# Attention and a gated feed-forward layer on one core: a sixth block of P per pair transposed by DMA, and the order of steps worked out anew

## The chip, the core and the metric

The kernel runs on one core of a Trainium2 chip. The core has a matrix engine (TensorE, PE in the profile; its weight loads are PEld), three elementwise engines (VectorE = DVE, ScalarE = ACT, GpSimd = POOL) and SyncE (SP), which in this kernel issues all DMA transfers. The five run side by side, each through its own instructions in order. The metric is the time of one execution on the device in microseconds (us), less is better.

## The reference

```
q_n, k_n = rmsnorm(q, g_q), rmsnorm(k, g_k)          # over head_dim
scores = (1 / sqrt(64)) * q_n @ k_n^T                # 8 batches x 12 heads, 448 x 448
attn = softmax(scores);  x = attn @ v                # heads joined: 8 x 448 x 768
h = relu(x @ w_in)                                   # 768 -> 1024
c[t] = cw[0]*h[t-1] + cw[1]*h[t] + cw[2]*h[t+1]      # three taps along the sequence
out = (h * sigmoid(c)) @ w_out                       # 1024 -> 768
```

All inputs of the attention are float32; the three weights of the second part arrive as 64-bit floats. The output is float32, 8 x 448 x 768.

## The kernel before

**Tiling.** Two heads make a pair, so there are 48 pairs, six for each batch. The 2 x 448 = 896 query rows of a pair are cut into seven blocks of 128 rows (`SLOTS`, `NS = 7`), numbered `j = 0..6` in the order in which they are worked on. Float32 values on the matrix path are split in two float16 halves, a high and a low one (`hi = cast(x)`, `lo = x - hi`), and a product is three float16 matmuls. Pairs 0 to 9 (`whole(n)`, `PH["nf"] = 10`) use float32 matmuls without the split.

**Steps of a pair.** `load_k`, `load_q`, `v_load` bring the data. `square`, `square_sum`, nine `rsqrt` steps and `apply_rms` (lines 385 to 441) normalise q and k. k, and q of the first ten pairs, are turned on TensorE (`qk_transpose`), evacuated and split; q of pairs from ten on is split first (`q_hi`, `q_lo`) and turned by a DMA transpose (`q_turn`). For each of the seven blocks `scores` does the matmuls, `soft_max` the row maximum on DVE, `soft_exp` the exponential on ACT with the row sum beside it. The result is P, 128 rows x 448 columns in float32, and P has to be turned, since P times V sums over the columns. There are two ways for it:

- on TensorE: `p_transpose` (line 686, four transposes into a PSUM bank), `p_evac` (cast of the bank to the high half, on ACT or DVE), `p_low` (line 702, the low half on DVE);
- by DMA: `p_hi` (cast to the high half in one of four buffers `ph`), `p_lo` (the low half, line 110), `p_turn` (line 678, one DMA transpose of both halves, SBUF to SBUF, issued by SP).

`nd(n)` says how many of the seven blocks go by DMA: none for pairs below `PH["n1"] = 10`, and `PH["nd"] = 5` for the others, since `PH["n2"] = 0`. So before, blocks 0 to 4 of pairs 10 to 47 go by DMA, 38 x 5 = 190 transposes, and blocks 5 and 6 go through TensorE. Both ways write the same tile `PT`, of which there are two; a `p_hi` needs a free one of the four `ph` buffers, that is, the transpose of four turns before has landed. `pv` (line 764) multiplies `PT` by the split V, `x_scale`, `x_hi`, `x_lo` divide by the row sums and split again. The row sums take a way of their own through DRAM (`sum_add` to `sum_load`, lines 709 to 729).

**Steps of a batch.** When the six pairs of a batch are there, `in_part` (line 848) multiplies by w_in, `in_relu`, `in_conv`, `in_tanh`, `in_gate`, `in_hi`, `in_lo` make the gated product, and `out_part` (line 917) multiplies by w_out.

**The order.** No step waits in source order: every step is entered in a plan with a due time (`at(t, fn, ...)`, shifted by `SHIFT`), what it needs (`needs`), and what it costs on each engine that may do it (`options`). Before the program is built, a planner goes through simulated time. For each engine it picks the step with the smallest sum of its earliest start and `beta` times its urgency, and it picks the engine where there is a choice (`on[step]`, with a patience `PH["p_..."]` for the second engine). `PH` holds the limits too: `nbulk`, how many bulk loads may be in flight, `cs`, `ct`, `cm`, how many PSUM banks each use may hold. The result is one fixed order for each engine. The times in `options` enter only this order; on the chip each engine runs its list in order and waits on semaphores.

```
key = t + sw + (BETA if e != "SP" else PH["sp"]) * urgency(step), urgency(step), steps[step][1]
if pick is None or key < pick[0]:
    pick = key, t, step
```

Of the kernel before, what the change touches and what calls it, by code (L numbers as in the profile page):

```python
# [17 lines left out]


PH = dict(  # L20
    sw=0.0, f_pl=0.0, f_ql=1.033, f_lo=0.063, f_rms=0.006, f_sq=0.0, T=17.289, ti=32.944,
    si=4.255, so=8.682, hop=0.426, beta=0.03, wi0=-31.45, wi1=127.539, wo0=29.304, wo1=182.047,
    cw=74.737, p_evac=1.025, p_hi=0.642, p_lo=3.777, p_rms=17.798, p_v=0.759, p_x=3.533,
    p_g=0.165, p_relu=0.299, p_cv=2.053, p_ev=3.086, sp=0.027, nbulk=6, p_rs=0.095, p_sq=3.551,
    p_w=3.55, v0=13.758, nd=5, cs=5, ct=4, cm=9, ne=5, n2=0, n1=10, q1=10, nf=10, pvs=4,
    p_sa=3.242, p_c0=3.399, p_ca=1.542, p_ss=0.242, p_qh=2.3, p_ql=2.401, p_ph=0.99, p_pl=1.378,
)
PACE = [
    17.644, 18.636, 16.286, 18.384, 14.587, 14.007, 12.166, 11.326, 21.435, 16.597, 21.428,
    21.065,  # L30
]
SHIFT = dict(
    prepare=-80.692, load_g=44.746, make_g=210.801, load_cw=-19.035, make_cw=387.553,
    load=41.371, convert=225.692, bound=365.257, bound_max=324.412, bound_turn=42.238,
    bound_row=76.875, bound_spread=4.635, scale=275.319, in_factor=440.833, split=103.321,
    rest=-2.799, out_factor=-0.968, load_k=306.569, load_q=-19.17, square=439.405,
    square_sum=329.986, rsqrt=54.627, apply_rms=238.269, qk_transpose=264.997, qk_hi=82.963,
    v_load=445.045, v_bound=-0.71, scores=57.55, soft_max=-4.441, soft_exp=50.335,
    p_transpose=316.253, p_evac=1.763, sum_add=226.657, sum_step=5.685, sum_transpose=51.88,
    sum_evac=233.745, sum_store=120.158, sum_load=1.259, pv=451.756, x_scale=158.975,  # L40
    x_hi=114.608, x_lo=5.331, v_max=-19.522, v_turn=600.483, v_row=7.16, v_spread=215.011,
    v_scale=11.299, qk_lo=-6.348, q_hi=-9.487, q_lo=109.312, q_turn=418.088, p_hi=567.012,
    p_lo=0.249, p_turn=241.201, p_low=3.084, v_hi=86.801, v_lo=289.452, moe_scales=90.042,
    in_part=33.426, in_relu=242.776, in_conv=118.288, in_tanh=106.186, in_gate=-5.208,
    in_hi=235.807, in_lo=15.201, in_carry=67.828, out_scales=27.298, out_part=423.396,
    out_evac=97.431, out_store=-1.54,
)
SCHED = {}
ON_ACT = ""
# [20 lines left out]
def tile_attention_moe(ctx: ExitStack, tc, q, k, v, g_q, g_k, w_in, conv_w, w_out, out):  # L70
# [15 lines left out]
    T = PH["T"]  # L86
# [79 lines left out]
    cw = cw_in if conv_w.dtype == F32 else const.tile([P, 3, NFC], F32, name="cw")  # L166
# [3 lines left out]
    wo = wo32.bitcast(F16).rearrange("p c (s e) -> p s c e", s=2)  # L170
# [438 lines left out]
    def nd(n):  # L609
        return 0 if n < PH["n1"] else PH["ne"] if n < PH["n2"] else PH["nd"]  # L610
# [663 lines left out]
    def options(name, *a):  # L1274
        n, wo = a[0] if a else None, a and a[0] == "out"
        n0 = a and isinstance(a[0], int) and a[0] < 2
        dma = lambda kind, c, k=1, g="C": ("ACT" if kind in ON_ACT.split() else "SP", c, (g, k))
        dve, act, pool, pe = (lambda c, e=e: (e, c, None) for e in ("DVE", "ACT", "POOL", "PE"))
        return dict(
            load=lambda: [dma("w", 1.5 if wo else 1.95)],  # L1280
            convert=lambda: [dve(0.55 if wo else 0.68)] if a[2] else [dve(0.35 if wo else 0.42)],
            bound=lambda: [act(0.6 if wo else 0.7)],
            bound_max=lambda: [dve(0.1)],
            scale=lambda: [dve(0.6)],
            split=lambda: [act(0.94 if wo else 1.15)],
            rest=lambda: [dve(1.01 if wo else 1.28), pool(3.9 if wo else 4.95)],
            in_factor=lambda: [dve(0.07)],
            out_factor=lambda: [dve(0.07)],
            load_g=lambda: [dma("g", 0.3, 4)],
            make_g=lambda: [dve(0.36)],  # L1290
            prepare=lambda: [dve(0.1)],
            load_cw=lambda: [dma("cw", 0.55)],
            make_cw=lambda: [dve(0.52)],
            load_k=lambda: [dma("lk", 0.82)],
            load_q=lambda: [dma("lq", 0.53, 2) if n % 2 else dma("lq", 1.05)],
            square=lambda: [act(1.06), pool(1.89)] if a[1] == 2 else [act(0.55), pool(1.05)],
            square_sum=lambda: [dve(1.21 if a[1] == 2 else 0.62)],
            rsqrt=lambda: [dve(0.19)] if a[1] == 1 or n0 and not a[2] else [dve(0.19), pool(0.47 if a[1] in (4, 7, 8) else 0.23)],
            apply_rms=lambda: [dve(0.69), pool(1.04)] if n0 else [pool(1.04), dve(0.69)],
            qk_transpose=lambda: [pe(0.42)],  # L1300
            qk_hi=lambda: [act(0.6), dve(0.62)],
            qk_lo=lambda: [dve(0.65)],
            q_hi=lambda: [act(0.62), dve(0.42), pool(0.61)],
            q_lo=lambda: [pool(1.15), dve(0.69)],
            q_turn=lambda: [("SP", 1.25, ("T", 1))],
            v_load=lambda: [dma("lv", 0.78)],
            v_bound=lambda: [dve(0.68)],
            v_max=lambda: [dve(0.3)],
            v_scale=lambda: [dve(0.7)],
            scores=lambda: [pe(0.77 if whole(a[0]) else 0.585)],  # L1310
            soft_max=lambda: [dve(0.62)],
            soft_exp=lambda: [act(0.73)],
            p_transpose=lambda: [pe(0.455)],
            p_low=lambda: [dve(0.63)],
            p_evac=lambda: [act(0.59), dve(0.62)],
            sum_add=lambda: [pool(0.3), dve(0.09)],
            sum_step=lambda: [dve(0.195)],
            sum_store=lambda: [dma("rd", 0.2)],
            sum_load=lambda: [dma("rb", 0.45)],
            pv=lambda: [pe(0.765 if nd(a[0]) else 8 * 0.00086 * S)],  # L1320
            x_scale=lambda: [dve(0.7 if nd(a[0]) else 0.85)],
# [24 lines left out]
            v_lo=lambda: [dve(0.75)],
            p_hi=lambda: [act(0.57), dve(0.39), pool(0.55)],
            p_lo=lambda: [pool(1.03), dve(0.61)],
            p_turn=lambda: [("SP", 1.25, ("T", 1))],
        )[name]()  # L1350

    PATIENCE = dict(
        qk_hi="hi", q_hi="qh", q_lo="ql", apply_rms="rms", x_hi="x", x_lo="lo", in_hi="g", in_lo="g",
        out_evac="ev", sum_add="sa", v_hi="hi", v_lo="lo", p_hi="ph", p_lo="pl", sum_evac="ev", v_bound="v", rest="w", rsqrt="rs", square="sq", convert="c0", in_relu="relu", in_conv="cv", p_evac="evac", in_carry="ca",
# [117 lines left out]
    while len(order) < len(steps):  # L1472
        best, free_banks = None, room()
        for e, ws in waiting.items():
            pick = None
            for step, (t, _, dma) in ws.items():
# [29 lines left out]
        _, c, dma = waiting[e][step]  # L1506
# [82 lines left out]
```

## Time and profile before

| | us |
|---|---|
| median of three runs | 846.53 (845.52 to 847.14) |
| the profiled execution | 847.59 |
| its span, first to last instruction | 845.8 |

The page of the profile gives the busy time of each engine over the span, the span in 40 slices, the DMA queues, the chain of work that ended last and the costliest groups of instructions. A group's line names the source line, engine, operation, written and read tiles, shapes and count; then its busy time and the mean duration of one in ns; then the idle time of the engine before them and who ended it. A table by stages gives, for each stretch of the span, the busy time of the engines, the granted clock of TensorE, and the share of the 16 DMA engines.

In 40 slices, the tenths of busy time of the engines and of the DMA:

```profile
PE   4897999999999999999999999999899999999998
DVE  6998999997999988897699997897899877883430
ACT  4988998898899888898899887898899887883541
POOL 1352665587787865877787864876788775862110
DMA  8954545259987899589986899589987997484001
```

The last three slices or so are the feed-forward part of the last batch alone, on TensorE.

### The profile page before, as it was taken

Reading aid. Unit: us, or ns where it says so; the run is one execution under the profiler, and the core shown is the slowest. Engines: PE = TensorE matmul, PEld = TensorE weight load, DVE = VectorE, ACT = ScalarE, POOL = GpSimd, SP = SyncE. Lnnn points to the kernel's source line nnn. Section 1 sums busy time; section 2 is a strip of 40 time slices with the busy share of each in tenths; the row PEclk is TensorE's granted clock in tenths of the full one; section 3 lists DMA queues with packets and bytes.
Section 4 is the critical chain, followed back from the end, with each engine's and each line's share of the span. In section 5 each row is a group of like instructions: output and inputs, shape, how many; then the busy total and the mean of one; then the engine's idle time right before and its main releaser. Section 6 shows DMA issues by size and latency. Waiting matters only on the chain.

```text
span 845.8 us, 17137 instructions
## 1 busy us (share of the span) xinstructions
PE 807.7 (95%) x5726; PEld 441.5 (52%) x5726; DVE 692.6 (82%) x1303; ACT 693.0 (82%) x1622; POOL 533.5 (63%) x649
## 2 busy tenths in 40 slices
PE   4897999999999999999999999999899999999998
PEld 2443545445555555555555555555555555555554
DVE  6998999997999988897699997897899877883430
ACT  4988998898899888898899887898899887883541
POOL 1352665587787865877787864876788775862110
PEclk9998999999999999999999999999999999999999
DMA  8954545259987899589986899589987997484001
GB/s 205 237 155 119 137 144 156 70 93 188 190 179 137 174 192 203 110 168 170 212 184 139 173 185 189 115 173 179 207 179 151 166 175 149 79 144 116 10 16 60
DMA packets 305576, 127.50 MB, mean 151 GB/s; under 512 B 245248, under 2 KB 301904, under 8 KB 305488
## 3 DMA queue, kind: packets, MB, share of 16 engines
q1 hardware_dynamic: 305488, 126.41, 71.8%
q8 instruction: 45, 0.74, 0.4%
q14 instruction: 43, 0.35, 0.2%
HBM read 56.65 MB, written 11.18 MB: 80 GB/s over the span
## 4 chain that ended last, share of the span: by engine, by line
PE 42%; DVE 22%; DMA 12%; ACT 10%; POOL 6%; issue 4%; SPq 3%; ACTq 0%; POOLq 0%; DVEq 0%
PE bank L848 15%; PE bank L917 13%; PE bank L764 5%; DMA PT<-ph 5%; PE bank L642 5%; PE bank L686 3%; DMA rB<-rd 2%; POOL ph L110 2%; DMA wo<-in_moe_w_in_dram 2%; DMA qkf<-in_q_dram 2%; POOL sq L110 2%; DVE st L396 1%; ACT ph L98 1%; DVE vp L748 1%; DVE PT L702 1%
## 5 line engine op out<-in xcount | busy, mean ns | idle before, releaser
L848 PE MATMUL bank<-x,wi 128*128 128x448 f16 x1152 | 233.4, 353 | 0.0
L917 PE MATMUL bank<-wo,gring 128*128 128x384 f16 (+1 forms) x1056 | 196.5, 327 | 0.0
L848 PEld LDWEIGHTS <-wi 128*128 128x128 f16 x1152 | 110.1, 98 | 101.6 <-issue 10.3
L642 PE MATMUL bank<-kT,qT 64*128 64x448 f16 (+3 forms) x1072 | 132.0, 395 | 4.0 <-ACT qT L98 2.6
L917 PEld LDWEIGHTS <-gring 128*128 128x128 f16 (+1 forms) x1056 | 101.6, 99 | 63.1 <-issue 8.8
L110 POOL TENSOR_TENSOR sq<-qkf,st 112x512 f32<-112x512 f32 x92 | 101.1, 1115 | 6.1 <-DVE st L417 5.0
L764 PE MATMUL bank<-PT,vp 112*64 112x448 f16 x912 | 93.5, 354 | 0.0
L110 POOL TENSOR_TENSOR x<-x,x 128x448 f16<-128x448 f32 x48 | 50.5, 1052 | 54.8 <-ACT x L98 53.9
L764 PEld LDWEIGHTS <-vp 112*64 112x64 f16 x912 | 48.5, 110 | 40.2 <-issue 10.8
L396 DVE TENSOR_REDUCE st<-sq 112x16 f32<-112x1024 f32 (+1 forms) x50 | 58.3, 1167 | 12.3 <-ACT sq L385 12.1
L702 DVE TENSOR_TENSOR PT<-bank,PT 112x512 f16<-112x512 f32 x76 | 51.5, 682 | 11.5 <-ACT PT L98 11.4
L642 PEld LDWEIGHTS <-qT 64*128 64x128 f16 (+1 forms) x912 | 33.3, 97 | 48.7 <-issue 27.3
L385 ACT ACTIVATE sq<-qkf 112x1024 f32<-112x1024 f32 (+1 forms) x47 | 48.2, 1025 | 11.7 <-DMA qkf<-in_q_dram 6.6
L98 ACT CAST PT<-bank 112x512 f16<-112x512 f32 x76 | 44.2, 583 | 3.9 <-PE bank L686 3.8
L917 PE MATMUL bank<-wo,wi 128*128 128x384 f16 (+1 forms) x192 | 46.9, 326 | 0.0
L456 PE MATMUL bank<-ident,sq 112*128 112x112 f32 x232 | 33.8, 270 | 13.6 <-DVE st L425 9.1
L748 DVE SCALAR_TENSOR_TENSOR vp<-v,vsc,vp 112x512 f16<-112x512 f32 x38 | 40.3, 1060 | 5.5 <-ACT vp L102 5.4
L110 POOL TENSOR_TENSOR qkf<-sq,qkf 112x512 f16<-112x512 f32 x35 | 42.3, 1209 | 0.2
L98 ACT COPY PT<-bank 112x512 f32<-112x512 f32 x69 | 39.5, 582 | 2.3 <-PE bank L686 2.1
L709 POOL TENSOR_SCALAR rsum<-rsum 128x7 f32<-128x7 f32 x48 | 14.5, 302 | 42.1 <-ACT e_(0_6_304 L656 10.7
L775 DVE TENSOR_TENSOR x<-bank,rB 128x448 f32<-128x448 f32 x38 | 23.5, 620 | 18.5 <-PE bank L764 11.8
L764 PE MATMUL bank<-PT,v 112*64 112x448 f32 x160 | 33.9, 568 | 3.6 <-ACT PT L98 3.4
(2228 smaller groups left out, 1972.9 us busy)
## 6 DMA issues: line engine op xcount, KB each, us to landing
qkf<-in_k_dram SPq DMA_DIRECT2D x48, 224.0 KB
v<-in_v_dram SPq DMA_DIRECT2D x48, 224.0 KB
rB<-rd SPq DMA_DIRECT2D x96, 112.0 KB
wo<-in_moe_w_in_dram SPq DMA_DIRECT2D x12, 512.0 KB
gring<-in_moe_w_out_dram SPq DMA_DIRECT2D x16, 384.0 KB
qkf<-in_q_dram SPq DMA_DIRECT2D x24, 224.0 KB
qkf<-in_q_dram SPq DMA_DIRECT2D x48, 112.0 KB
PT<-ph SPq DMA_TRANSPOSE x190
```

Source lines behind the costliest of these rows:

```text
L98: (nc.scalar.copy if e == "ACT" else elementwise(e).tensor_copy)(dst, src)
L110: elementwise(e).tensor_tensor(dst, a, b, op=op)
L385: nc.scalar.activation(sq, x, AF.Square)
L396: nc.vector.tensor_reduce(st, sq, axis=AX.X, op=ALU.add)
L456: nc.tensor.transpose(ps[:, t * PB : (t + 1) * PB], x[:, t], ident[:PB, :PB])
L642: nc.tensor.matmul(ps[u][o, :S], lhs, rhs, start=(i == 0), stop=(whole(m) or i == 2),)
L686: nc.tensor.transpose(ps[:PB, kt * P : (kt + 1) * P], e[:, kt * PB : (kt + 1) * PB], ident)
L702: nc.vector.tensor_tensor(turned(n, j, 1), held["t", ("p", n, j)][:PB].rearrange("p (k q) -> p k q", k=NB), turned(n, j, 0), op=ALU.subtract,)
L748: nc.vector.scalar_tensor_tensor(vp[:, 1], old("v", n), old("vsc", n // NP)[:PB, 1:2], vp[:, 0], op0=ALU.mult, op1=ALU.subtract,)
L764: nc.tensor.matmul(ps[HALF[h], :S], lhs, rhs, start=(i == 0 and k == 0), stop=(i == pvs(n)[-1] and k == NB - 1),)
L848: nc.tensor.matmul(ps[:, :S], wi[:, wl, c, fc * P : (fc + 1) * P], old("x", b * NP + c)[:, xl], start=(i == 0), stop=(i == 3 * NP - 1),)
L917: nc.tensor.matmul(ps[p0 : p0 + m, :NO2], g, wo[:, wl, fc, half * NO2 : (half + 1) * NO2], start=(i == 0), stop=(i == 3 * NFC - 1),)
```

## The change

`PH["nd"]` goes from 5 to 6 (and `ne`, which no pair uses while `n2 = 0`): block 5 of pairs 10 to 47 takes `p_hi`, `p_lo`, `p_turn` in place of `p_transpose`, `p_evac`, `p_low`. Block 6 stays on TensorE. Beside it the figures of `options` are set to other durations, and all numbers of `PH`, `PACE` and `SHIFT`, from which the planner makes its order, are new. No function is added, and no computation changes.

```diff
 PH = dict(
-    sw=0.0, f_pl=0.0, f_ql=1.033, f_lo=0.063, f_rms=0.006, f_sq=0.0, T=17.289, ti=32.944,
-    si=4.255, so=8.682, hop=0.426, beta=0.03, wi0=-31.45, wi1=127.539, wo0=29.304, wo1=182.047,
+    sw=0.0, f_pl=0.0, f_ql=0.616, f_lo=0.065, f_rms=0.079, f_sq=0.356, T=17.368, ti=37.602,
+    si=4.258, so=8.922, hop=0.87, beta=0.015, wi0=-40.604, wi1=121.264, wo0=30.91, wo1=183.564,
...
-    p_g=0.165, p_relu=0.299, p_cv=2.053, p_ev=3.086, sp=0.027, nbulk=6, p_rs=0.095, p_sq=3.551,
-    p_w=3.55, v0=13.758, nd=5, cs=5, ct=4, cm=9, ne=5, n2=0, n1=10, q1=10, nf=10, pvs=4,
+    p_g=6.911, p_relu=3.009, p_cv=2.979, p_ev=1.037, sp=0.047, nbulk=3, p_rs=0.08, p_sq=9.733,
+    p_w=34.001, v0=27.558, nd=6, cs=5, ct=4, cm=8, ne=6, n2=0, n1=10, q1=10, nf=10, pvs=4,
...
-            load=lambda: [dma("w", 1.5 if wo else 1.95)],
-            convert=lambda: [dve(0.55 if wo else 0.68)] if a[2] else [dve(0.35 if wo else 0.42)],
+            load=lambda: [dma("w", 1.55 if wo else 2.03)],
+            convert=lambda: [dve(0.58 if wo else 0.73)] if a[2] else [dve(0.38 if wo else 0.45)],
...
-            load_g=lambda: [dma("g", 0.3, 4)],
+            load_g=lambda: [dma("g", 0.6, 4)],
...
-            make_cw=lambda: [dve(0.52)],
+            make_cw=lambda: [dve(2.1)],
...
-            v_load=lambda: [dma("lv", 0.78)],
+            v_load=lambda: [dma("lv", 0.85)],
...
-            soft_exp=lambda: [act(0.73)],
+            soft_exp=lambda: [act(0.645)],
...
-            moe_scales=lambda: [dve(0.34)],
-            out_scales=lambda: [dve(0.2)],
+            moe_scales=lambda: [dve(0.5)],
+            out_scales=lambda: [dve(0.35)],
...
-            in_gate=lambda: [dve(0.675)],
+            in_gate=lambda: [dve(0.625)],
...
-            v_lo=lambda: [dve(0.75)],
+            v_lo=lambda: [dve(0.8)],
...
-            p_lo=lambda: [pool(1.03), dve(0.61)],
+            p_lo=lambda: [pool(1.06), dve(0.64)],
```

The other changed figures move by 0.3 us or less. All twelve numbers of `PACE` and all of `SHIFT` are different; they are due times, which enter the order by the small factor `beta`.

More of the change, by code (lines that the diff above doesn't have):

```diff
@@ L20 @@
 PH = dict(
-    sw=0.0, f_pl=0.0, f_ql=1.033, f_lo=0.063, f_rms=0.006, f_sq=0.0, T=17.289, ti=32.944,
-    si=4.255, so=8.682, hop=0.426, beta=0.03, wi0=-31.45, wi1=127.539, wo0=29.304, wo1=182.047,
-    cw=74.737, p_evac=1.025, p_hi=0.642, p_lo=3.777, p_rms=17.798, p_v=0.759, p_x=3.533,
-    p_g=0.165, p_relu=0.299, p_cv=2.053, p_ev=3.086, sp=0.027, nbulk=6, p_rs=0.095, p_sq=3.551,
-    p_w=3.55, v0=13.758, nd=5, cs=5, ct=4, cm=9, ne=5, n2=0, n1=10, q1=10, nf=10, pvs=4,
-    p_sa=3.242, p_c0=3.399, p_ca=1.542, p_ss=0.242, p_qh=2.3, p_ql=2.401, p_ph=0.99, p_pl=1.378,
+    sw=0.0, f_pl=0.0, f_ql=0.616, f_lo=0.065, f_rms=0.079, f_sq=0.356, T=17.368, ti=37.602,
@@ L27 @@
+    si=4.258, so=8.922, hop=0.87, beta=0.015, wi0=-40.604, wi1=121.264, wo0=30.91, wo1=183.564,
+    cw=109.431, p_evac=0.582, p_hi=0.601, p_lo=1.803, p_rms=0.055, p_v=0.692, p_x=0.554,
+    p_g=6.911, p_relu=3.009, p_cv=2.979, p_ev=1.037, sp=0.047, nbulk=3, p_rs=0.08, p_sq=9.733,
+    p_w=34.001, v0=27.558, nd=6, cs=5, ct=4, cm=8, ne=6, n2=0, n1=10, q1=10, nf=10, pvs=4,
+    p_sa=0.344, p_c0=0.115, p_ca=3.233, p_ss=3.597, p_qh=0.9, p_ql=1.02, p_ph=2.577, p_pl=1.839,
 )
 PACE = [
-    17.644, 18.636, 16.286, 18.384, 14.587, 14.007, 12.166, 11.326, 21.435, 16.597, 21.428,
@@ L30 @@
-    21.065,
+    19.442, 19.21, 17.334, 19.007, 12.781, 14.556, 11.946, 10.5, 24.531, 17.632, 21.413, 16.555,
 ]
 SHIFT = dict(
[L33 to L43, printed above, removed]
@@ L44 @@
-    in_part=33.426, in_relu=242.776, in_conv=118.288, in_tanh=106.186, in_gate=-5.208,
-    in_hi=235.807, in_lo=15.201, in_carry=67.828, out_scales=27.298, out_part=423.396,
-    out_evac=97.431, out_store=-1.54,
+    prepare=50.409, load_g=80.485, make_g=139.084, load_cw=25.457, make_cw=234.685, load=30.589,
+    convert=97.397, bound=220.055, bound_max=507.005, bound_turn=123.413, bound_row=60.465,
+    bound_spread=116.886, scale=370.991, in_factor=592.715, split=131.171, rest=-5.431,
+    out_factor=40.976, load_k=212.269, load_q=-21.899, square=440.332, square_sum=336.161,
@@ new lines @@
+    rsqrt=38.568, apply_rms=519.452, qk_transpose=522.906, qk_hi=86.859, v_load=335.971,
+    v_bound=-6.083, scores=-3.276, soft_max=-4.535, soft_exp=22.477, p_transpose=365.286,
+    p_evac=1.005, sum_add=351.05, sum_step=2.117, sum_transpose=98.65, sum_evac=268.147,
+    sum_store=195.738, sum_load=7.047, pv=359.863, x_scale=83.997, x_hi=231.104, x_lo=6.104,
+    v_max=-20.799, v_turn=500.58, v_row=107.465, v_spread=217.607, v_scale=141.469,
+    qk_lo=-5.749, q_hi=-16.553, q_lo=85.951, q_turn=369.086, p_hi=542.574, p_lo=-4.723,
@@ L47 @@
+    p_turn=306.823, p_low=-2.298, v_hi=186.072, v_lo=212.059, moe_scales=126.571,
+    in_part=119.565, in_relu=322.051, in_conv=207.454, in_tanh=32.888, in_gate=3.629,
+    in_hi=191.919, in_lo=13.049, in_carry=212.144, out_scales=193.212, out_part=272.943,
+    out_evac=259.647, out_store=1.003,
 )
@@ L1297, in options @@
             square_sum=lambda: [dve(1.21 if a[1] == 2 else 0.62)],
-            rsqrt=lambda: [dve(0.19)] if a[1] == 1 or n0 and not a[2] else [dve(0.19), pool(0.47 if a[1] in (4, 7, 8) else 0.23)],
-            apply_rms=lambda: [dve(0.69), pool(1.04)] if n0 else [pool(1.04), dve(0.69)],
+            rsqrt=lambda: [dve(0.19)] if a[1] == 1 or n0 and not a[2] else [dve(0.19), pool(0.54 if a[1] in (4, 7, 8) else 0.28)],
+            apply_rms=lambda: [dve(0.69), pool(1.07)] if n0 else [pool(1.07), dve(0.69)],
             qk_transpose=lambda: [pe(0.42)],
@@ L1329, in options @@
             in_tanh=lambda: [act(0.58)],
-            in_gate=lambda: [dve(0.675)],
+            in_gate=lambda: [dve(0.625)],
             in_hi=lambda: [act(0.57), dve(0.39), pool(0.55)],
             in_lo=lambda: [pool(1.03), dve(0.61)],
-            in_carry=lambda: [dve(0.18), act(0.29)],
+            in_carry=lambda: [dve(0.3), act(0.29)],
             out_part=lambda: [pe(0.67)],
```

2 lines of the change are left out of this document (1 added, 1 removed).

## The prediction

> **What bounds the kernel now.** I read the page's busy times first, then one table of busy time by stage (start 0 to 80 us, the ten whole pairs to about 180, the long middle to 780 in which all 38 transposed pairs run, the end), then the waits of TensorE.
>
> ```profile
> PE 807.7 (95%) x5726; PEld 441.5 (52%) x5726; DVE 692.6 (82%) x1303; ACT 693.0 (82%) x1622; POOL 533.5 (63%) x649
> ...
> 0.00:80.00 80.00, 58.25 (x311) 30.81 (x313) 66.69 (x157) 60.20 (x147) 23.16 (x53) 0.94 0.74 184
> 80.00:180.00 100.00, 96.25 (x563) 49.23 (x563) 98.02 (x188) 91.55 (x221) 62.16 (x75) 1.00 0.43 114
> 180.00:780.00 600.00, 590.82 (x4454) 326.30 (x4451) 511.84 (x936) 517.78 (x1213) 438.81 (x513) 1.00 0.84 166
> 780.00:845.80 65.80, 62.34 (x406) 35.13 (x403) 16.06 (x25) 23.47 (x42) 9.32 (x9) 1.00 0.08 28
> ...
> PE bank L456 <- DVE st L425: 9.1, 1, 9.1
> ...
> PE bank L198 <- DVE mx L193: 2.3, 2, 2.1
> PE bank L686 <- ACT e_(12_5_2417 L656: 1.3, 1, 1.3
> ```
>
> The columns of a stage row are its length, then busy time of PE, PEld, DVE, ACT and POOL, then TensorE's granted clock, the DMA share and GB/s. In the middle TensorE works 590.8 of 600 us and idles 9.2. Its worst wait in the whole run, 9.1 us, is the very first one; in the middle the worst are a reduction of 2.3 us in total and one exponential of 1.3. No other engine comes near: ACT has 517.8 of 600, DVE 511.8, POOL 438.8. So TensorE sets the pace of the middle, and what it is spared there is worth its full length as long as nothing else becomes late. In the start it idles 80 - 58.25 = 21.75 us, in the second stage 3.75, at the end 65.8 - 62.34 = 3.46, all together 845.8 - 807.65 = 38.2 us.
>
> **The change: TensorE.** From pair ten on the sixth block of P leaves the path p_transpose, p_evac, p_low and takes p_hi, p_lo, p_turn. That is 38 blocks (pairs 10 to 47), each four TensorE transposes less.
>
> ```profile
> 180.00:780.00 600.00, 45.41 (x304) 34.43 (x304) 1.00 0.84 166
> ...
> 608.92 0.60 PE L686 MATMUL bank<-ident,e_(37_5_8049 128*112 128x128 f32 x4
> 609.36 0.73 PE L848 MATMUL bank<-x,wi 128*128 128x448 f16 x3
> ...
> 611.45 0.60 PE L686 MATMUL bank<-ident,e_(37_6_8060 128*112 128x128 f32 x4
> 611.98 2.46 PE L764 MATMUL bank<-PT,vp 112*64 112x448 f16 x24
> ```
>
> The first row is line 686 alone in the middle: 304 matmuls, that is 76 blocks, busy 45.41 us or 0.60 a block. Part of it lies under the next matmul, so the slot is better read from start to start: 609.36 - 608.92 = 0.44 us, and 611.98 - 611.45 = 0.53 us where P times V follows. I take the mean, 0.48: 38 x 0.48 = **18.2 us less**. Bounds: 38 x 0.44 = 16.7 and 38 x 0.60 = 22.7. All matmuls that use P, the scores and the feed-forward part stay as they are.
>
> **The other engines.** Removed: 38 casts on ACT and 38 subtractions on DVE. Added: 38 p_hi and 38 p_lo.
>
> ```profile
> L98 ACT CAST PT<-bank 112x512 f16<-112x512 f32 x76 | 44.2, 583 | 3.9 <-PE bank L686 3.8
> L702 DVE TENSOR_TENSOR PT<-bank,PT 112x512 f16<-112x512 f32 x76 | 51.5, 682 | 11.5 <-ACT PT L98 11.4
> ...
> 180.00:780.00 600.00, 5.26 (x7) 97.89 (x178) 198.95 (x191) 1.00 0.84 166
> ```
>
> The last row is everything that writes the two halves of P for the DMA: 178 of the 190 p_hi stand on ACT at 97.89 / 178 = 0.55 us, and POOL has nearly all of p_lo at 198.95 / 191 = 1.04. If the new ones are placed alike, ACT changes by 38 x (0.55 - 0.58) = -1, DVE by -38 x 0.68 = -26, POOL by +38 x 1.04 = +40 us. The middle, 582 us long by then, would hold ACT 517, DVE 486, POOL 479. None of the three reaches TensorE's 573, so these edits cost nothing by their length. What covers them is the slack of ACT, 82 us now and 65 then; if it is gone, they cost up to the whole gain, which is a rival below.
>
> **The DMA engines and SP.** 38 DMA transposes more.
>
> ```profile
> 160.00:163.00 3.00, 2.11 (x13) 1.15 (x13) 3.00 (x7) 2.65 (x7) 0.00 (x0) 1.00 0.41 78
> 425.50:429.00 3.50, 3.50 (x21) 1.84 (x20) 3.50 (x7) 3.32 (x9) 3.31 (x6) 1.00 1.25 194
> ...
> L678 SPq DMA_TRANSPOSE PT<-ph x190: 1231/1272/2526, 176.1 to 770.9; - x190
> ...
> q1 hardware_dynamic: 305488, 126.41, 71.8%
> ...
> SPq L723 <- ACT rT L98: 48.3, 20, 4.7
> ```
>
> From 160 to 163 us the core's traffic is one such transpose with a tiny store, and the 16 engines show 0.41 x 3 = 1.23 us of work. So 38 of them are 38 x 1.23 = 47 us. The middle now has 0.84 x 600 = 504 us; it would have 551 in 582, a share of 0.95. The share counts packets that overlap: from 425.5 to 429 it is 1.25 with TensorE busy throughout. So 0.95 is not a wall, but a quarter of the room up to 1.25 is used (0.11 of 0.41), and transfers will land later. Each transpose holds SP's queue 1.27 us, 48 us in all, and everything behind it in that queue (loads of q, k and v, the row sums' round trip, stores of the result) starts that much later. SP has room: it spends 48 us of the middle waiting for the row sums on ACT alone. I cost the traffic at 4 us of new TensorE idle: ACT's casts now wait 21.6 us for earlier transposes (row below), 38 more of the same kind make it 21.6 x 228 / 190 = 25.9, and I let all of the 4.3 reach TensorE. Bounds: 0, and the whole 18.
>
> The page VectorE: DVE Perf Modes of the Trainium skill, in The three transpose paths and Rules for kernel authors, speaks against the change: it gives 390 ns for a 128x128 transpose on TensorE and 1309 on the DMA path, and says to use TensorE where a PSUM destination will do. By its figures alone (an estimate from that page, four tiles on the one path and eight on the other) the move exchanges 1.6 us for 10.5. This trace has 0.48 for 1.23, so the direction agrees and the ratio does not, and what decides here is who has room.
>
> **Order and planner figures.** The new parameters change no operation, only which step comes when; in a fixed order per engine that can make any wait longer or shorter. Loads in flight, for one, are held to three and no longer to six (nbulk), so fewer loads lie ahead of a transpose, and each load comes closer to its use. One corrected figure shows its kind: the planner held ACT 0.73 us for an exponential, now 0.645.
>
> ```profile
> 428.63 0.63 ACT L656 ACTIVATE e_(26_3_5525<-bank,sst_(26_3_5494 128x448 f32<-128x448 f32 x1
> 429.16 0.19 ACT L656 ACTIVATION_READ_ACCUMULATOR e_(26_3_5525<-bank,sst_(26_3_5494 128x1 f32 x1
> 429.25 0.62 ACT L656 ACTIVATE e_(26_4_5535<-bank,sst_(26_4_5503 128x448 f32<-128x448 f32 x1
> ```
>
> Two exponentials follow each other in 429.25 - 428.63 = 0.62 us, so the new figure is the truer one. Its worth is bounded by the idle time there is: the middle can give at most 9.2 us, the start 25.5 less the 9.1 before its first data. As an order can also lose that much, I take 0, and let the start give or lose some 4 us inside the range.
>
> **Sum.** 845.8 - 18.2 + 4.3 = 831.9 us of span. The profiled execution took 847.59 us, 1.8 above its span, and the median of the three runs, 846.53, is 1.06 below that: 831.9 + 1.8 - 1.06 = 832.6. I say **832 us**.
>
> **Rivals.**
>
> *ACT takes over, and half of the gain is lost.* ACT's load alternates between batches of six pairs, about 93 us each:
>
> ```profile
> 553.00:647.00 94.00, 91.39 (x678) 50.62 (x677) 81.92 (x156) 86.02 (x203) 73.20 (x87) 1.00 0.90 175
> 647.00:740.00 93.00, 92.71 (x726) 51.13 (x721) 78.03 (x140) 78.56 (x183) 68.55 (x80) 1.00 0.79 148
> ...
> ACT ph L98 <- DMA PT<-ph: 21.6, 28, 2.1
> ```
>
> In the first of these ACT is busy 86.0 of 94 us and has 8.0 idle; TensorE's cut of 6 x 0.48 = 2.9 leaves it 5.1. If its waits there don't shrink, that batch is as long as before. Half of the batches are such, so half of 18.2 is lost, and with the 4.3 of new idle the time is 846.5 - 9.1 + 4.3 = **842 us**. For it: the DMA share in the same batch is 0.90, the highest. Against it: much of ACT's idle time is there because TensorE is late, and the order is made anew with ACT's true figure.
>
> *Slower: late transposes stop ACT.* The place is the ring of four buffers for the halves of P: a p_hi on ACT waits until the transpose of four turns before has landed, and behind it in ACT's order stand exponentials, casts of k and x and the activations of the feed-forward part, for which DVE, POOL and then TensorE wait. Today that is 21.6 / 190 = 0.11 us a turn. ACT's other idle time in the middle is 82.2 - 21.6 = 60.6 us; if half of it is forced, the middle lasts 517 + 30 + the ring's waits, which equals today's 600 at 53 us, or 0.23 us a turn, twice today's. From there each further hundredth is 2.3 us; at 0.27 the middle is 609 and the time **856 us**. For it: 0.95 of DMA share, and the largest single wait of 2.1 us. Against it: a share of 1.25 did not stop TensorE.
>
> A long gap would cost TensorE a second time, by its clock:
>
> ```profile
> 45.41 3.23 PE L764 MATMUL bank<-PT,v 112*64 112x448 f32 x16
> ...
> 60.00:80.00 20.00, 13.30 (x65) 7.27 (x65) 17.63 (x33) 16.08 (x39) 3.07 (x4) 0.83 0.43 118
> ...
> 72.05 4.89 PE L764 MATMUL bank<-PT,v 112*64 112x448 f32 x16 [3.02 <-ACT PT L98]
> ```
>
> The same sixteen matmuls take 3.23 us, and 4.89 after a gap of 3.02, in the stretch whose granted clock is 0.83. TensorE: Matmul & The Clock Gate of the Trainium skill, Part 1, says the clock halves after an idle window of about 3.4 us; these rows agree that gaps of this size cost it, and in the middle (clock 1.00) no gap of today's is that long.
>
> *More than forecast.* No new idle at all, the slot worth its full 0.60, or a better start: 846.5 - 22.7 = **824 us** or less.
>
> **How the numbers follow.** Chances: the forecast (825 to 838) 0.62, ACT takes over (838 to 846) 0.20, slower 0.11, more than forecast 0.07. The range is 824 to 846: from the upper bound of the slot with no new idle to the loss of the whole gain; it leaves out the slower case and most of the last, under 0.2. A measurement of this kernel tells about 0.2% from no change, so "faster" is below 844.8 and "slower" above 848.2. Faster: 0.62 + 0.07 + some 0.13 of the second case = 0.82; same 0.07; slower 0.11.
>
> **What would show it.** Line 686 with 152 matmuls fewer in the middle and TensorE's busy time near 789; 228 DMA transposes of P; line 702 with 38 subtractions and DVE near 667; POOL near 573; a DMA share of 0.95 in the middle with TensorE idle 9 to 15 us there. The rivals show as growing waits of ACT's p_hi for the transposes (over 26 us, over 50 for the slower one), with TensorE's idle time in the middle above 18. Idle time before 80 us far from 22 would mean that the order, not the blocks, moved the time.

## The result, and the profile after

| | us |
|---|---|
| kernel before, median of four runs beside it | 846.02 (843.16 to 847.14) |
| changed kernel, median of four runs | 855.87 (852.3 to 857.17) |
| ratio | 1.0115, 95% interval 1.0074 to 1.0156 |
| the changed kernel's profiled execution, and its span | 856.75, 854.8 |

The change made the kernel slower, by 9.85 us between the medians; 832 had been forecast. First the page's busy times of the changed kernel, and its table by the stages of the prediction (length, then PE, PEld, DVE, ACT, POOL, the granted clock, the DMA share, GB/s):

```profile
PE 795.1 (93%) x5574; PEld 423.2 (50%) x5574; DVE 705.6 (83%) x1296; ACT 692.0 (81%) x1630; POOL 540.5 (63%) x664
```

```profile
0.00:80.00 80.00, 60.26 (x329) 31.09 (x329) 70.57 (x169) 64.93 (x157) 28.41 (x55) 0.96 0.75 199
80.00:180.00 100.00, 95.37 (x580) 50.59 (x579) 96.11 (x191) 95.59 (x232) 59.39 (x81) 1.00 0.46 120
180.00:780.00 600.00, 568.29 (x4201) 301.32 (x4200) 522.50 (x913) 506.73 (x1199) 442.39 (x520) 1.00 0.92 178
780.00:854.80 74.80, 71.21 (x469) 40.16 (x467) 16.43 (x25) 24.72 (x45) 10.35 (x10) 1.00 0.13 40
```

The 152 matmuls are gone and TensorE is busy 12.6 us less (795.1 for 807.7). But it idles 59.7 us in place of 38.2, and the stages say where: 19.7 in the start (21.75 before), 4.6 in the second stage, 3.6 at the end, and **31.7 in the middle, where it was 9.2**. The granted clock there is still 1.00. VectorE, from which 38 subtractions were taken, is busy 13 us more.

The waits of the changed kernel (who waited for whom: us in total, times, longest), of all engines and then of SyncE:

```profile
POOL ph L109 <- ACT ph L97: 65.4, 73, 3.9
ACT ph L97 <- DMA PT<-ph: 39.9, 44, 4.1
DVE x L774 <- DMA rB<-rd: 22.0, 16, 2.6
PE bank L685 <- ACT e_(32_6_6935 L655: 2.7, 1, 2.7
...
SPq L677 <- POOL ph L109: 56.5, 50, 3.6
```

The same waits of the kernel before, as far as the prediction does not show them:

```profile
POOL ph L110 <- ACT ph L98: 74.8, 69, 4.3
DVE x L775 <- DMA rB<-rd: 4.6, 6, 1.1
...
SPq L678 <- POOL ph L110: 21.8, 26, 2.4
```

ScalarE waits 39.9 us for a landed transpose (21.6 before). VectorE waits 22.0 us (4.6 before) for the row sums' round trip through DRAM, whose loads stand in SyncE's queue between the transposes. SyncE itself stands 56.5 us (21.8 before) with a transpose whose low half GpSimd has not written yet. TensorE's longest single wait of the middle, 2.7 us, is for the exponential of block 6 of pair 32; block 6 is the one block that TensorE still transposes. It is no single case: 17 waits of the middle, 16.5 of the 31.7 us, are for the exponential of some block 6 (two waits, 0.4 us, before). The chain of work that led up to that one, and the instructions of GpSimd and VectorE at the time, show how such a wait is made (the chain: start, length, what; then the timeline: start, length, engine, line, instruction):

```profile
516.01 3.21 DMA rB<-rd
...
521.00 0.60 DVE vacc L542
521.60 0.85 DVE vp L747
522.46 1.44 DVE qkf L109
523.90 1.45 DVE sq L109
...
528.33 4.49 DVE vsc L830
...
533.49 0.54 DVE sst_(32_6_6921 L647
```

```profile
527.21 1.60 POOL L109 TENSOR_TENSOR qkf<-sq,qkf 112x512 f16<-112x512 f32 x1
528.25 4.56 DVE L830 TENSOR_TENSOR vsc<-vsc,wsc 128x1 f32<-128x1 f32 x1
528.77 1.03 POOL L109 TENSOR_TENSOR ph<-e_(32_3_6775,ph 128x448 f16<-128x448 f32 x1
529.76 1.03 POOL L109 TENSOR_TENSOR ph<-e_(32_4_6794,ph 128x448 f16<-128x448 f32 x1
530.76 1.04 POOL L109 TENSOR_TENSOR ph<-e_(32_5_6826,ph 128x448 f16<-128x448 f32 x1
531.75 1.03 POOL L109 TENSOR_TENSOR gring<-c_(4_0_6833,gring 128x448 f16<-128x448 f32 x1
```

Read it backwards. TensorE has nothing to transpose before block 6's exponential, that waits 2.75 us for its row maximum, and the maximum stands in VectorE's queue behind a product of 128 x 1 numbers that takes 4.56 us. That product begins while GpSimd writes one tile, and it ends at 532.81, 0.03 us after the end of the fourth instruction that GpSimd then ran without a gap; the third of these four is the low half of block 5, which the change added. VectorE was behind already: it had waited for rB. The Trainium skill says in SBUF — State Buffer, Who interferes with whom, that VectorE and GpSimd share one pair of ports to SBUF, which is an exclusive lock. These rows agree, and in them VectorE did not get the ports between GpSimd's instructions. That is not so every time: the same product at 498.83 us was through in 0.63 us, although GpSimd's next instruction followed without a gap.

```profile
498.83 0.63 DVE L830 TENSOR_TENSOR vsc<-vsc,wsc 128x1 f32<-128x1 f32 x1
```

### The profile page after: what moved, and what is told of

Read it like the earlier page. It is cut to its first block, busy times and chain, and to the rows that moved or that the text cites. A ratio compares the mean times of both kernels' runs of the same rounds, so it can differ in the third digit from the quotient of the medians.

```text
span 854.8 us, 17037 instructions
## 1 busy us (share of the span) xinstructions
PE 795.1 (93%) x5574; PEld 423.2 (50%) x5574; DVE 705.6 (83%) x1296; ACT 692.0 (81%) x1630; POOL 540.5 (63%) x664
## 4 chain that ended last, share of the span: by engine, by line
DVE 23%; PE 22%; ACT 21%; DMA 13%; POOL 8%; issue 8%; SPq 4%; ACTq 0%; POOLq 0%; DVEq 0%
PE bank L916 11%; DMA PT<-ph 6%; PE bank L847 5%; POOL ph L109 4%; DMA rB<-rd 4%; ACT ph L97 3%; PE bank L641 2%; PE bank L763 2%; DVE sq L109 2%; SPq L677 2%; ACT PT L97 2%; DVE st L395 2%; POOL sq L109 1%; ACT sq L384 1%; DVE vp L747 1%
## 5 line engine op out<-in xcount | busy, mean ns | idle before, releaser
L916 PE MATMUL bank<-wo,gring 128*128 128x384 f16 (+1 forms) x1056 | 200.8, 327 | 1.7 <-DVE PT L701 0.9
L641 PE MATMUL bank<-kT,qT 64*128 64x448 f16 (+3 forms) x1072 | 129.7, 389 | 2.6 <-DVE c_(4_6_7303 L877 0.9
L109 POOL TENSOR_TENSOR x<-x,x 128x448 f16<-128x448 f32 x48 | 54.6, 1137 | 57.2 <-ACT x L97 56.8
L109 POOL TENSOR_TENSOR sq<-qkf,st 112x512 f32<-112x512 f32 x61 | 68.9, 1138 | 5.8 <-DMA qkf<-in_k_dram 2.4
L763 PEld LDWEIGHTS <-vp 112*64 112x64 f16 x912 | 50.5, 110 | 42.2 <-issue 14.8
L384 ACT ACTIVATE sq<-qkf 112x1024 f32<-112x1024 f32 (+1 forms) x49 | 50.3, 1026 | 3.8 <-DMA qkf<-in_q_dram 2.2
L109 DVE TENSOR_TENSOR sq<-qkf,st 112x512 f32<-112x512 f32 x35 | 45.0, 1289 | 0.1
L455 PEld LDWEIGHTS bank<-ident,sq 112*128 112x128 f32 x232 | 25.5, 143 | 28.9 <-POOL sq L109 16.3
L97 ACT CAST x<-x 128x448 f16<-128x448 f32 x45 | 25.4, 565 | 17.0 <-DVE x L774 14.2
L855 ACT ACTIVATE bank<-bank 128x448 f32<-128x448 f32 x64 | 34.1, 532 | 6.0 <-PE bank L847 5.4
```

Of the source, the lines that this page charges most:

```text
L97: (nc.scalar.copy if e == "ACT" else elementwise(e).tensor_copy)(dst, src)
L109: elementwise(e).tensor_tensor(dst, a, b, op=op)
L384: nc.scalar.activation(sq, x, AF.Square)
L455: nc.tensor.transpose(ps[:, t * PB : (t + 1) * PB], x[:, t], ident[:PB, :PB])
L641: nc.tensor.matmul(ps[u][o, :S], lhs, rhs, start=(i == 0), stop=(whole(m) or i == 2),)
L763: nc.tensor.matmul(ps[HALF[h], :S], lhs, rhs, start=(i == 0 and k == 0), stop=(i == pvs(n)[-1] and k == NB - 1),)
```

## Experiments: the order and its figures

Every time below is beside runs of the kernel before on the same chip (medians 845.88 to 847.13). A difference between the medians of two kernels here is good to 3 or 4 us. The planned end is the planner's own, which the kernel works out while it is built: 832.5 us before (13.3 short of the span) and 819.7 after (35.1 short). The distance from the planned end to the span is what I call the lag.

**Five blocks with the new numbers, and six with the old.**

```diff
 five_new: all numbers of PH, PACE, SHIFT and options as changed, but
-    ... nd=6, cs=5, ct=4, cm=8, ne=6
+    ... nd=5, cs=5, ct=4, cm=8, ne=5
 six_old: all numbers as before, but nd=6, ne=6
```

> All new figures of the change (PH, PACE, SHIFT, options), but five blocks by DMA as before; the planner makes a new order. Its own simulated end is 837.2 us (832.5 for the kernel before, 819.7 for the changed one, whose spans on the chip are 845.8 and 854.8: the chip lags the plan by 13.3 and by 35.1 us). Theory T1, the sixth transpose (late transposes, or their traffic) makes the lag: the lag is about that of before or less, 5 to 13 us, span 842 to 850, and ACT waits about 20 us for transposes. Theory T2, the new order and its placements (apply_rms on DVE, for one) make the lag whatever the number of blocks: the lag stays near 35, span 865 to 875.

> Only the sixth block: nd=6 with all figures of before; the planner makes a new order, simulated end 849.1 us. T1: the lag is that of the changed kernel or more, 30 to 40 us, span 879 to 889. T2: the lag is about that of before, 13 to 18, span 862 to 867.

five_new: 854.65 us, ratio 1.0092 (1.0064 to 1.0119), span 852.3, planned 837.2, so a lag of 15.1. six_old: 875.9 us, 1.0345 (1.0283 to 1.0407), span 876.2, planned 849.1, lag 27.1. Neither came into a range that was written for it. Both are slower than before, by more than their plans say; that the numbers were tuned together with the number of blocks is the likely reason, and is not shown. But the lag sorts them: 13 to 15 us with five blocks, 27 to 35 with six, whichever the figures.

**One parameter by 2%, and the RMS products back on GpSimd.** In the changed order 35 of these products stand on VectorE, at 1289 ns, where the plan has 690 (before: 4 at 692 ns, the rest on GpSimd).

```profile
L109 POOL TENSOR_TENSOR sq<-qkf,st 112x512 f32<-112x512 f32 x61 | 68.9, 1138 | 5.8 <-DMA qkf<-in_k_dram 2.4 <-ACT sq L384 1.6 <-issue 0.5
L109 DVE TENSOR_TENSOR sq<-qkf,st 112x512 f32<-112x512 f32 x35 | 45.0, 1289 | 0.1
```

```diff
 near_beta:
-    si=4.258, so=8.922, hop=0.87, beta=0.015,
+    si=4.258, so=8.922, hop=0.87, beta=0.0147,
 poolrms:
-            apply_rms=lambda: [dve(0.69), pool(1.07)] if n0 else [pool(1.07), dve(0.69)],
+            apply_rms=lambda: [dve(0.69), pool(1.07)] if n0 else [pool(1.07)],
```

> The changed kernel with one parameter of the order moved by 2% (beta 0.015 to 0.0147), nothing else: the planner's own end rises from 819.7 to 831.6 us, VectorE's and GpSimd's shares stay about the same. If the planned end carries over to the chip, this kernel takes 864 to 870 us. If the last 12 us of the plan are an accident of one order that the chip does not follow, it takes 852 to 860 us, the lag falling from 35 to about 24.

> The changed kernel with the RMS product (apply_rms) given to GpSimd alone from pair two on, as nearly all were before, and the order worked out anew: planned end 825.4 us against 819.7. If VectorE's 35 products at 1.29 us, planned at 0.69, make the lag, it falls by about 20 us and the time is 840 to 846. If the lag regresses with the plan's own gain (the chosen order is the lowest of many, others are truer), the time stays at 852 to 860 although the plan is 6 us worse.

near_beta: 866.54 us, 1.0223 (1.0192 to 1.0254); its plan is 11.9 us longer, its time 10.7. poolrms: 865.38, 1.0211 (1.0179 to 1.0244), above both of its ranges; plan 5.7 longer, time 9.5. So in these two cases a worse plan with six blocks was a slower kernel. Their lags are 32.3 us (span 863.9) and 36.0 (861.4), about that of the changed kernel. The lag is therefore no error that only the best plan of many has, and the products on VectorE do not make it. What the products alone cost is not measured, since poolrms has another order.

**The corrected figure of the exponential.** The change plans soft_exp at 0.645 us, which is its ACTIVATE alone; to the end of the accumulator's read it is 0.72 us, as the old figure 0.73 had it (429.16 + 0.19 - 428.63 in the prediction's rows). In no_acc that read is left out, so that the step is as short as the new figure says.

```diff
-            new("rsum", n, [P, NS], F32)
+            rings.setdefault("rsum", Ring(BUFS["rsum"])).put(("rsum", n), rsbuf[n % 2])   # ones
...
-            accum_out=old("rsum", n)[:, c : c + 1],
```

> The changed kernel in its own order, with the exponentials' row sums left out (no accumulator is read; the sums are set to one). Each soft_exp then takes about what the new figure says (0.645 us) in place of 0.723. If the wrong figure made the order run late, the time falls by 8 to 12 us, to 844 to 848, and the lag of the middle from 34 to about 25. If the lag is elsewhere, 0 to 3 us (853 to 856).

> The kernel before in its own order, with the same sums left out. Its order was made with 0.73 us, the true length, so a shorter step should win little by the theory of the wrong figure: 0 to 3 us (843 to 846). If ScalarE simply bounds both kernels, it falls as much as the changed one.

no_acc: 854.4 us, 1.0082 (1.005 to 1.0114). before_no_acc: 849.36, 1.0016 (0.9994 to 1.0039). The gain of 1.5 us (2.8 if the two ratios are compared) cannot be told from zero, and the theory of the wrong figure needed 8 to 12; it falls.

## Experiments: what the sixth block costs in the changed order

The order of steps on each engine is the changed kernel's in all of these; instructions are only left out, so the plan's 819.7 is the same. In no_sixth, no_turn6 and turn5_eighth the tile `PT` also stands in two fixed buffers that GpSimd clears at the start. No run has that alone; TensorE idles 20.7 to 22.2 us in the start of these three, for 19.7 in the changed kernel, so there it costs them a little.

```diff
 no_sixth: p_hi, p_lo and p_turn
+        if j == 5:
+            return            # its place in P cleared once, in pairs 10 and 11
 no_turn6: the same in p_turn alone      no_lo6: in p_lo alone
 no_hi6: p_hi takes its buffer, but leaves the copy out for j == 5
 no_casts6: no_lo6 and no_hi6 together
 turn5_eighth:
-            places(n)...[:, :, c * P : (c + 1) * P],
+            places(n)...[:, : (1 if j == 5 else 8), c * P : (c + 1) * P],   # input alike
```

> The changed kernel in its own order of steps, but the DMA transpose of the sixth block moves only the first of its eight 128x128 pieces, so the low half and three quarters of the high half of that block of P are left out; PT stands in two fixed buffers, cleared once. 38 transposes are an eighth as long, all instructions stay in their places. T1: the ring's waits of ACT (39.9 us) fall to about 20 and the span to 832 to 840. T2: the span stays at 848 to 856, within 6 us of the changed kernel.

> The changed kernel in its own order, with the sixth block's two casts and its DMA transpose left out (38 pairs; its place in P stays zero). TensorE's work is unchanged. If the sixth block's chain (its transfers, its casts, the ring of four buffers between them) makes the middle run behind the plan, the lag of the middle falls from 34 to near 10 us and the time to 830 to 836. If the lag belongs to the order itself (steps packed so close that any error of a duration is passed on), only what the transfers and the cast cost is won: 3 to 7 us, time 848 to 853.

> The changed kernel in its own order, with the sixth block's low cast (38 on GpSimd at 1.07 us) left out, its transfer kept. If GpSimd's added work and the stretch that it puts on VectorE's SBUF work make the lag, the time falls by 10 us or more, to 846 or less. If it is the transfers, or the order, it falls by 0 to 4 us (852 to 856).

> The changed kernel in its own order, with the sixth block's high cast left out on ScalarE (its buffer keeps an older block's), low cast and transfer kept. If ScalarE's work and its wait for a free buffer carry the sixth block's price, the time falls by 10 us or more, to 846 or less. If the price is spread over the chain, it falls by 2 to 5 us (851 to 854).

> The changed kernel in its own order, with the sixth block's DMA transpose left out (its place in P stays zero) and both its casts kept. If SyncE's queue carries the price (38 issues of 1.35 us = 51 us, behind which the other loads, sums and transposes of one queue stand), the time falls by 12 to 18 us, to 838 to 844, and VectorE's wait for rB shrinks. If the transfer's data is all that counts, it falls by 3 to 5 us as with an eighth of the data (851 to 853).

> The changed kernel in its own order, with both casts of the sixth block left out and its DMA transpose kept (it turns what an older block left in the buffer). If the casts add up one by one (0.9 + 5.6), it takes 848 to 851 us. If the two as a pair carry all that the transposes do not (21.6 - 8.5 = 13), it takes 841 to 845 us. Then SyncE also stops waiting for GpSimd at these transposes.

| run | left out of block 5, 38 pairs | median | less than 855.87 | ratio to before |
|---|---|---|---|---|
| no_hi6 | high cast (ACT) | 855.0 | 0.9 | 1.0092 (1.0065 to 1.0119) |
| turn5_eighth | 7/8 of the transpose's data | 852.47 | 3.4 | 1.0067 (1.0039 to 1.0095) |
| no_lo6 | low cast (POOL) | 850.25 | 5.6 | 1.0037 (1.0023 to 1.0051) |
| no_casts6 | both casts | 847.52 | 8.4 | 1.0003 (0.9986 to 1.002) |
| no_turn6 | the transpose | 847.33 | 8.5 | 1.0011 (0.9994 to 1.0029) |
| no_sixth | all three | 834.26 | 21.6 | 0.9841 (0.9816 to 0.9865) |

Taken from the ratios, each against runs of the kernel before on its own chip, the six differences are 1.9, 4.1, 6.6, 9.5, 8.8 and 23.2 us in the order of the table, good to some 4 or 5. The first two can't be told from zero. Only no_sixth came into a range that was written for it; turn5_eighth (by its span of 847.0) and no_casts6 missed one by 1 us or less, and no_hi6, no_lo6 and no_turn6 fell between theirs or outside.

**The whole.** Without the sixth block's chain the changed order takes 834.26 us, 11.8 less than the 846.02 of the kernel before (12.9 less than the runs beside it, 847.13); its span of 831.6 is 11.9 above the plan, a lag as with five blocks. So the order keeps to its plan once the chain is out of it, TensorE's saving is real, and the chain that takes TensorE's place costs 21.6 us in this order. The stage row of no_sixth, then those of no_turn6 and no_casts6:

```profile
180.00:780.00 600.00, 588.96 (x4359) 314.23 (x4357) 508.50 (x925) 498.65 (x1180) 410.15 (x489) 1.00 0.83 164
```

```profile
180.00:780.00 600.00, 581.04 (x4308) 309.14 (x4303) 526.75 (x920) 511.92 (x1210) 447.88 (x527) 1.00 0.83 164
```

```profile
180.00:780.00 600.00, 577.36 (x4276) 306.92 (x4276) 504.02 (x917) 493.72 (x1169) 405.08 (x484) 1.00 0.93 180
```

TensorE idles 11.0, 19.0 and 22.6 us of the middle, for 31.7 in the changed kernel.

**The transposes: data and queue.** An eighth of the data brings the DMA share of the middle from 0.92 to 0.82 (row below) and wins 3.4 us; taking the transfer out of the queue brings it to 0.83 and wins 8.5. The two intervals don't meet, so some 5 us are not data.

```profile
180.00:780.00 600.00, 578.04 (x4262) 307.84 (x4264) 515.81 (x915) 509.02 (x1204) 445.39 (x524) 0.99 0.82 165
```

SyncE's transposes by their line (duration ns least/median/longest), of the changed kernel, of turn5_eighth, of no_turn6:

```profile
L677 SPq DMA_TRANSPOSE PT<-ph x228: 1231/1263/2930, 164.0 to 781.1; - x114
```

```profile
L680 SPq DMA_TRANSPOSE pt<-ph x228: 1115/1250/2444, 165.1 to 773.0; - x114
```

```profile
L682 SPq DMA_TRANSPOSE pt<-ph x190: 1231/1248/2578, 167.4 to 766.4; - x190
```

With 38 of 228 at an eighth the median stays at 1250, and even the shortest holds the queue 1115 ns. Counted alone in the trace (every sixth of the row), the 38 small ones have a median of 1.33 us, and the 38 whole ones in the same place of the changed kernel 1.33 too. So what a transpose costs SyncE does not hang on its size here: about 38 x 1.25 = 48 us of queue were still there in turn5_eighth and are gone in no_turn6. Summed over the trace, SyncE's issuing instructions fill 487 of the 600 us of the middle (448 in the kernel before, 486 in turn5_eighth, 435 in no_turn6). The waits behind the transposes, first of turn5_eighth, then of no_turn6:

```profile
ACT ph L97 <- DMA pt<-ph: 28.5, 34, 2.7
DVE x L777 <- DMA rB<-rd: 19.2, 13, 3.0
...
ACT ph L97 <- DMA pt<-ph: 16.5, 23, 2.2
DVE x L779 <- DMA rB<-rd: 10.3, 10, 2.0
```

ScalarE waits 39.9 us for a buffer in the changed kernel, 28.5 with an eighth of the data and 16.5 without the transpose; VectorE waits 22.0, 19.2 and 10.3 for rB. Without the transpose the queue is shorter, and a buffer is also free again without a landing. No run changes one of the two alone, so how the 5 us divide between queue and buffers is not shown.

**The casts: GpSimd and VectorE.** The busy times of no_lo6:

```profile
PE 794.4 (94%) x5574; PEld 423.3 (50%) x5574; DVE 689.3 (81%) x1296; ACT 692.0 (82%) x1630; POOL 501.5 (59%) x626
```

38 instructions fewer on GpSimd (39 us) and none fewer on VectorE: its 1296 instructions, the same ones, are busy 689.3 us in place of 705.6. Each microsecond of low casts had lengthened VectorE's work by 0.4. The other profiles of this order with the same 1296 bear it out: with the low cast VectorE is busy 701 to 712 us, without it (no_sixth, no_casts6) 690.2 and 685.6. The product of 4.56 us shows how. In no_lo6 GpSimd's row ends one instruction earlier at that place, since block 5's low half is missing and the next instruction waits for ScalarE, and the product takes 2.57 us:

```profile
527.03 2.57 DVE L832 TENSOR_TENSOR vsc<-vsc,wsc 128x1 f32<-128x1 f32 x1
```

The high cast alone is worth nothing that can be told from zero, and both together 8.4. In no_casts6 ScalarE still waits 46.3 us for buffers, and the DMA share of the middle is 0.93: the 8.4 us are won with both as high as in the changed kernel.

**What is left.** 8.5 and 8.4 make 16.9 of 21.6. The other 4.7 may be what two delays in one chain cost together, or the uncertainty of four medians, which is as large. TensorE's idle time in the single profiles leaves no such rest (12.7 + 9.1 = 21.8 for 20.7), but no_turn6's profiled execution was 2.9 us faster than its median. That stays open.

## Experiments: the ring of buffers, the stores, a new search

**Six buffers in place of four.** The two more lie in a part of the expert weights' tile that is free from pair ten on; the gate values give up the two places they had there.

```diff
+    rest_i = wi32[:, DM // P].bitcast(F16).rearrange("p (i a k q) -> p i a k q", i=2, a=2, k=4)
+    phs = phbuf + [rest_i[:, i] for i in range(2)]
...
-    gspot = [gring[:, i] for i in range(NGR)] + spots(wi32[:, DM // P]) + spots(wo32[:, NFC])
...
+    gspot = [gring[:, i] for i in range(NGR)] + spots(wo32[:, NFC])
...
-        ph = ring.put(("ph", (n, j)), phbuf[ring.count % BUFS["ph"]])
+        ph = ring.put(("ph", (n, j)), phs[ring.count % 6])
```

> The changed kernel in its own order, with six buffers of casts (ph) in place of four, the two more in a part of the expert weights' tile of which the gate values (gring) now use two places fewer (14 of 16). If the ring of four makes the sixth block's chain late, ScalarE's ph waits fall from 39.9 to under 8 us and the time to 838 to 845. If the casts' and transfers' own work makes the lag, those waits go too and the time stays at 851 to 856.

850.5 us, 1.0057 (1.0038 to 1.0077), 5.4 less, between its two ranges. The two new buffers go by the name `wi` in the trace. ScalarE's casts no longer wait for `ph` and 3.1 us for `wi`, in place of 39.9; GpSimd's wait for ScalarE falls from 65.4 us to 33.5 and 2.5:

```profile
POOL ph L109 <- ACT ph L97: 33.5, 47, 2.5
ACT wi L97 <- DMA PT<-wi: 3.1, 8, 0.9
POOL wi L109 <- ACT wi L97: 2.5, 8, 0.5
DVE x L779 <- DMA rB<-rd: 24.0, 14, 3.3
```

So ending nearly all of the 39.9 us of waits for buffers is worth 5.4. The sixth block is still dear when its casts hardly wait for a buffer: the kernel stays 4.1 us above the runs of the kernel before beside it.

Three runs before this one had put the two buffers where two of the sixteen gate places lie, so that gate values were overwritten and casts also waited for the readers of the gate. They tell nothing about the ring:

> The changed kernel in its own order, with six buffers of casts (ph) in place of four from pair ten on; the two more lie in a part of the expert weights' tile that is free by then. If the ring of four is what makes the sixth block's chain late (ScalarE waits for a landed transfer before it may cast again, and its exponentials wait behind it), ScalarE's ph waits fall from 39.9 to under 8 us and the time to 838 to 845. If the casts' and transfers' own length makes the lag, the waits go too but the time stays at 851 to 856.

> The kernel before in its own order, with the same six buffers of casts. Its ScalarE waits 21.6 us for ph, but TensorE idles only 9.2 us in its middle. By both theories little: the waits fall under 5 us, the time by 0 to 4 us (842 to 846).

> The changed kernel with six buffers of casts, of which the planner is told, and the order worked out anew with the same parameters: planned end 824.8 us. If the ring of four was the lag, the chip follows this plan as it does five blocks (13 to 16 us behind): 838 to 842 us. If the lag lies in the casts and transfers, it stays at 30 to 35: 855 to 860 us.

They took 854.52, 849.1 and 855.26 us.

**Fewer stores.** Of the result's stores of batches 0 to 6, only 16 of each 128 rows are written.

```diff
+        m = P if b == 7 else 16
-            outf[row0 : row0 + P, half * NO2 : (half + 1) * NO2],
+            outf[row0 : row0 + m, half * NO2 : (half + 1) * NO2],
```

> The changed kernel in its own order, but of each of the result's stores of batches 0 to 6 only 16 of 128 rows are written: some 8 MB of the 137 MB of DMA traffic are left out, about 30 us of the 16 engines' time, two thirds of what the sixth transposes add, without a change to any transpose. T1 in the form 'traffic': the span falls by 8 us or more, to 847 or less. T1 in the form 'ring and latency', and T2: it stays within 3 us of 854.

852.96 us, 1.0068 (1.0037 to 1.0099): 2.9 less, where the theory of traffic had 8 or more. With turn5_eighth this speaks against the amount of traffic as the main price.

**An order searched anew.** For research6 I fitted the planner's costs to the runs so far, and searched its parameters with them, with six buffers.

```diff
-            soft_exp=lambda: [act(0.645)],      p_turn, q_turn 1.25,   p_hi [act(0.57), ...
+            soft_exp=lambda: [act(0.725)],      p_turn, q_turn 1.3,    p_hi [act(0.6), ...
-        dma = ... c, (g, k))
+        dma = ... 1.2 * c, (g, k))
-            end = t + c
+            end = t + c + (0.04 if e == "POOL" and shared(e, step[0]) else 0.0)
```

> Six blocks, six buffers of casts, and an order searched anew with costs that fit the runs so far: soft_exp 0.725, a DMA transpose 1.3 in place of 1.25, every other DMA 1.2 times its figure, GpSimd's work on the shared port 0.04 longer, p_hi 0.6. With these costs the orders of the kernels before and after come out at 846 and 852 us, and this one is planned at 836.1 us. If these costs are what the old plan lacked, it takes 834 to 842 us. If a search only finds what a planner has wrong, 848 to 856 us.

854.43 us, 1.0096 (1.0069 to 1.0124), span 853.7 for a plan of 836.1. With these costs the plans of the kernels before and after come out at 846 and 852 us, near their spans; the new order still ran 17.6 us behind its plan. That the search went where the costs are wrong fits this, and one search shows no more. No kernel that computes the whole beat the one before.

## Why the prediction was wrong, step by step

- **TensorE's 18.2 us: right in kind, nearly in size.** no_sixth's page has TensorE busy 791.0 us, 16.7 less than before, and its time is 11.8 below (12.9 beside its own runs). That most of a TensorE saving shows as time is what the prediction's first part said.

```profile
PE 791.0 (95%) x5574; PEld 422.1 (51%) x5574; DVE 690.2 (83%) x1296; ACT 674.9 (81%) x1592; POOL 508.3 (61%) x630
```

- **"These edits cost nothing by their length": the step that failed most.** The condition, that the new steps are placed alike, failed too (VectorE came to 705.6 us, not 667, with 35 RMS products moved to it, and GpSimd to 540.5, not 573), but poolrms, with these products back on GpSimd, lags as much. The argument itself was wrong: it compared each engine's sum in the middle with TensorE's, and held 65 us of slack to be cover. Both casts together cost 8.4 us, and the low cast stretches VectorE's work by 16 us, which the sum left out.
- **"I cost the traffic at 4 us": mis-sized by half.** It measured 8.5 in no_turn6. The data is some 3.4 of it; the 4.3 stood for the waits of ScalarE's casts alone, and the near match says little. The other 5 us come from what the prediction dismissed with "SP has room", 48 us more in SyncE's queue, or from buffers that come free later; which of the two is not shown. That SyncE's 48 us of waiting come at other times than its new work is likely, and not shown either. The 1.23 us of one transpose was read off a transpose of q, 112 rows where P has 128: by the shares of the middle, 0.92 and 0.83 in no_turn6, the 38 are some 54 us of the DMA engines and not 47.
- **The rest, up to 4.7 us,** may come where both fall together, if it is real at all. The prediction added its terms as if each had slack of its own.
- **"The new figure is the truer one": wrong,** as the accumulator's read belongs to the step, and the planner takes 0.1 us for overlap off by itself. Its price of 1.5 us can't be told from zero.
- **"I take 0" for the order: not contradicted.** The start's idle time is 19.7 us for 21.75, and no_sixth lags its plan as the kernel before does. For the rest, near_beta shows what an order is worth: 10.7 us for 2% of one parameter. The prediction's range had 4 us for that, in the start alone.
- **The slower rival gave 856 us, and 855.87 came, but by its mechanism only in part.** The signs of the rivals came: ScalarE's ph waits above 26 us, TensorE's idle time in the middle above 18. But these waits are 39.9 us and not the 53 from which the rival was to decide, and six buffers, which end nearly all of them, win 5.4. So the match of the number is luck. The chain that it named runs on through places that it did not name: the ports that GpSimd shares with VectorE, and perhaps SyncE's queue.

Put together from the medians: 846.0 - 11.8 (the order with six blocks and no chain) + 8.5 (transposes) + 8.4 (casts) + 4.7 (open) = 855.8. The last term is what the others leave, so that the sum closes is no proof.

## What to carry to other kernels

Before moving work from the bounding engine to a chain of four others, count every queue that the chain passes (casts, issue, landing, buffer), not the sums of busy time: engines at 73 to 86% with fixed orders can still hand their delays to the one at 98%. In this kernel a DMA transpose held its issuing queue as long with an eighth of the data as with all of it, so count transposes there, not bytes. To price such a move, leave the new chain out of the finished order and then each of its parts; it took one run here to show that the saving was real, and a few more to divide most of the cost.

## What the runs showed of the hardware that was not expected

- A VectorE product of 128 x 1 numbers took 4.56 us while GpSimd ran one instruction to its end and four more without a gap. The eight of that line took 1274 ns on average: two took 4.56 and 3.72 us, the other six 0.14 to 0.63. Taking 38 GpSimd instructions away shortened the same VectorE work by 16.3 us.

```profile
L830 DVE TENSOR_TENSOR vsc<-vsc,wsc 128x1 f32<-128x1 f32 x8 | 10.2, 1274 | 0.0
```

- A DMA transpose held SyncE's queue as long for one tile of 128 x 128 as for eight (medians of 38 in the same place: 1.33 us each); the shortest of all, one of the small ones, took 1.115 us, and the shortest whole one of P 1.231.
